# Sparse attention feeding an MLP mixer: the global part of PV on 64 by 64 quarters, PV tiles in pairs, leftovers and first transposes at other places of a period

## The chip, the cores and the metric

The kernel runs on one core of a Trainium2 chip. The metric is the device time of one execution in microseconds (us). The core has a matrix engine, TensorE (PE, with its weight loads shown apart as PEld), and three engines that work on tiles: VectorE (DVE), ScalarE (ACT) and GpSimd (POOL). SyncE (SP) issues most of the DMAs. PE's results land in PSUM, from where DVE and ACT take them to SBUF.

## What is computed

Eight batches of 576 tokens go through attention with eight heads of 64 numbers. A token sees the tokens within 32 places, eight global tokens see and are seen by all. The result, 576 by 512 per batch, goes through a token-mixing MLP and a channel-mixing MLP.

```python
scores = scale * np.matmul(q, k.transpose(0, 1, 3, 2))
mask = np.abs(pos[:, None] - pos[None, :]) <= window
mask = mask | is_global[:, None] | is_global[None, :]
scores = np.where(mask, scores, -1000000000.0)
attn = np.exp(scores - max); attn = attn / (sum + 1e-09)
x = np.matmul(attn, v)                       # heads side by side: 576 x 512
h = np.maximum(x.T @ w_tok1, 0.0) @ w_tok2   # tokens mixed: 576 -> 256 -> 576
u = x + h.T
out = u + np.maximum(u @ w_ch1, 0.0) @ w_ch2 # channels mixed: 512 -> 1536 -> 512
```

## The kernel before

**Tiles.** The 576 tokens of a batch are five token tiles, four of 128 and one of 64. Scores are kept with keys on partitions and queries in columns, in strips of 64 keys that cover a band, so that the exponentials (`e_all`) are the stationary operand of the product with V. Heads are handled in four pairs p. A batch's attention has these steps, with their lines:

- `cast_qk` (ACT, L386 and L383) makes 16-bit copies of q and k. `T(b, p)` (PE, L400) transposes a pair's q and k into one PSUM tile `pT`, and DVE copies it out as `qT` (L406) and `kT` (L412). `TR(b)` (PE, L427) does the same for the leftovers, the last 64 tokens of all heads, in PSUM tile `pr`, copied out at L438. `globals_` (L392) puts the global queries beside `qT`.
- `S_` (PE, L458) makes the scores of a pair in two PSUM tiles, ACT takes the exponential (L470), `SM` (DVE, L476 and L481) applies the masks.
- `GK` and `LX` make `lf`: 128 rows, 16 per head, against all tokens, the part of the attention that goes through global tokens. `OG` (L539, L544) makes its other operand `rf`: the same 128 rows by 8 heads x 66 columns. `rf` is zero outside a head's own 16 rows, so rows 0 to 63 hold heads 0 to 3 and rows 64 to 127 heads 4 to 7.
- `PV(b, tau)` forms token tile tau of the attention: for each half of the heads (`hf`), a global product `lf` by `rf` (L656, 264 columns), then the local products `e_all` by V (L665, 66 columns for each of four heads), all for two strips of 64 queries (`tiles`), one in each half of PE's columns. The fifth tile has one strip only. 66 columns are 64 of V, one of ones whose sum is the denominator, and one of padding. DVE takes the reciprocal (L678) and divides (L679) into `x`.

The mixer's steps are `M1` (L692, five parts `ch` over the token tiles, then ACT makes `a`), `M2` (L716, three parts; DVE adds x and writes `u`, L721, or `ul`, L724), `M3` (a DMA transpose of `u` on SP, L733), then the dense products `M4` (L754, `b1p`, ACT makes `b`, L757) with `M4l` (L767) for the fifth tiles of two batches together, and `M5` (L780, `op`; DVE adds, L784, SP stores).

**PSUM.** Three pools: `pss` has two slots of two banks, `psv` one slot of two banks, `psm` two slots of one bank. A tile waits for a slot's earlier user to be read. Scores, `a1p` of M1, `hp` of M2 and most transposes come from `pss`; GK, OG and even PV tiles from `psv`; M4 and M5 from `psm`.

**Order.** The order of work on each engine is the order in which the program calls these functions; nothing reorders it. The program runs in periods b = 0 to 7. Period b works off the dense products M4 and M5 of batch b, and beside them, in two halves, the attention end of batch n = b+1 (PV, M1, M2, M3) and the attention beginning of batch m = b+2 (casts, TR, T, S_, SM, GK, OG). `first_half` and `second_half` write the order of periods 2 to 6 by hand: a list in which each `D` stands for the next dense unit (one M4, four matmuls of 512 columns) and the rest are the steps named above. In `first_half`, `c(k)` are two casts, `pv(tau)` is PV(n, tau), `tt(p)` is T(m, p) with its copies. Periods 0 and 1 have their own lists (`period_0`, `sparse2`); in period 0 the PV tiles of batch 1 already stand in pairs. Period 6 has no batch m, period 7 is dense work alone.

Of the kernel before, what the change touches and what calls it, by code (L numbers as in the profile page):

```python
# [9 lines left out]
F16 = mybir.dt.float16  # L10
# [5 lines left out]
P = 128  # L16
# [5 lines left out]
HQ = 64  # L22
ES = QS * NT - HQ
VW = 66
# [20 lines left out]
def kernel(  # L45
# [13 lines left out]
    B, H, S, D = q.shape  # L59
# [4 lines left out]
    NP = H // 2  # L64
# [14 lines left out]
    def pss(shape, dtype=F32, name="s"):  # L79
        return psS.tile(shape, dtype, tag="s", name=name)  # L80
# [252 lines left out]
    def gather_t(t):  # L333
        pg = (psm if t == 0 else psv)([P, 2, P], F16, name=f"pg_{t}")
        for ti in range(2):
            if t > 0:
                nc.vector.tensor_copy(out=g16[ti][t], in_=g32[ti][t])
            nc.tensor.transpose(out=pg[:, ti, :], in_=g16[ti][t], identity=ident)
        st[0]["gt", t] = pg
        if t > 0:  # L340
            GTE(t)
            GKE(t)
# [45 lines left out]
    def casts(b):  # L388
        return [lambda ti=ti, p=p: cast_qk(b, ti, p, nc.scalar.copy) for p in (None, 0, 1, 2, 3) for ti in range(2)]
# [4 lines left out]
        )  # L394

    def T(b, p):
        pT = (psm if b in (0, 2) else pss)([P, 2, 512], F16, name=f"pT_{b}_{p}")
        for ti, n in enumerate((qn, kn)):
            for i in range(4):
                nc.tensor.transpose(  # L400
                    out=pT[:, ti, P * i : P * i + P], in_=n[b % 2][:, i, 2 * p : 2 * p + 2, :], identity=ident
                )
        st[b]["pT", p] = pT
# [15 lines left out]
        TEk(b, p)  # L419

    def TR(b):
        pr = (psm if b in (0, 2) else pss)([P, 2, 4, NP * 16], name=f"pr_{b}")
        sel = ident.rearrange("p (n r x) -> p r n x", n=NP, r=2)
        for ti, n in enumerate((qr, kr)):
            for i in range(4):
                for par in range(2):
                    nc.tensor.matmul(  # L427
                        pr[64 * par : 64 * par + 64, ti, i, :], lhsT=n[b % 2][:, i, :], rhs=sel[:, par], start=True, stop=True
                    )
        st[b]["pr"] = pr  # L430
        if b > 0:
            TRE(b)

    def TRE(b, tis=(0, 1), eng=nc.vector.tensor_copy):
        for ti in tis:
            v_ = st[b]["pr"][:, ti].rearrange("p i (n x) -> p n x i", n=NP)
            dst = qTs[b % 2][:, :, NT - 1, NG : NG + LAST] if ti == 0 else kTs[b % 2][:, :, WIN + 512 : WIN + S]
            eng(out=dst.rearrange("p n (x i) -> p n x i", i=4), in_=v_)  # L438
# [208 lines left out]
    def PV(b, tau):  # L647
        s = st[b]

        sh = 64 if tau == NT - 1 and b % 2 == 1 else 0  # L650
        tiles = ((2 * tau, 0), (2 * tau + 1, 64)) if tau < NT - 1 else ((2 * tau, sh),)
        ps = (pss if b != 2 and tau % 2 else psv)([P, 2, 512], name=f"pv_{b}_{tau}")

        def glob(hf):
            for t, r0 in tiles:
                nc.tensor.matmul(  # L656
                    ps[r0 : r0 + 64, hf, 0 : NP * VW], lhsT=s["lf"][:, HQ * t : HQ * t + HQ],
                    rhs=s["rf"][:, 2 * hf : 2 * hf + 2], start=True, stop=False,
                )

        def local(hf, hh):
            h = NP * hf + hh
            for t, r0 in tiles:
                lo = QS * tau + (NG + HQ if t % 2 else NG)
                nc.tensor.matmul(  # L665
                    ps[r0 : r0 + 64, hf, VW * hh : VW * hh + VW], lhsT=e_all[:, h, lo : lo + HQ],
                    rhs=(vod if t % 2 else vsh)[b % 2][:, tau, h, :],
                    start=False, stop=hh == NP - 1,
                )

        for hf in range(2):
            glob(hf)
            for hh in range(NP):
                local(hf, hh)
        r = slice(0, P) if tau < NT - 1 else slice(sh, sh + 64)
        pq = ps[:, :, 0 : NP * VW].rearrange("p f (h x) -> p f h x", h=NP)
        rr = tiny.tile([P, 2, NP], F32, tag="rr", name=f"rr_{b}_{tau}")
        nc.vector.reciprocal(out=rr[r], in_=pq[r, :, :, D])  # L678
        nc.vector.tensor_tensor(  # L679
            out=x16s[b % 2][r, tau, :].rearrange("p (f h x) -> p f h x", f=2, h=NP), in0=pq[r, :, :, 0:D],  # L680
            in1=rr[r].unsqueeze(3).to_broadcast([P if tau < NT - 1 else 64, 2, NP, D]), op=ALU.mult,
        )

    def M1(b, ch):
        s = st[b]
        if ch == 0:
            ps = pss([P, 2, 512], name=f"a1p_{b}")
            s["a1p"], s["a1pp"] = [ps[:, 0], ps[:, 1]], ps
        ps = s["a1p"]
        for tt in range(2):  # L690
            w = w1[:, ch, P * tt : P * tt + P] if ch < NT - 1 else w1l[:, b % 2, P * tt : P * tt + P]
            nc.tensor.matmul(ps[tt], lhsT=w, rhs=x16s[b % 2][:, ch, :], start=(ch == 0), stop=(ch == NT - 1))  # L692
        if ch < NT - 1:
            return
        a1 = mb.tile([P, 2, DM], F16, tag="a1", bufs=1, name=f"a1_{b}")
        if b == 1:
            nc.scalar.activation(out=a1[:, 0], in_=s["a1pp"][:, 0], func=AF.Relu)
            nc.vector.tensor_scalar(out=a1[:, 1], in0=s["a1pp"][:, 1], scalar1=0.0, scalar2=None, op0=ALU.max)
        else:
            nc.scalar.activation(out=a1, in_=s["a1pp"], func=AF.Relu)  # L700
        s["a1"] = a1
        s["u16"] = mb.tile([P, 4, DM], F16, tag="u16", name=f"u16_{b}")
        if b % 2 == 0:
            s["ul"] = mb.tile([P, DM], F16, tag="ul", name=f"ul_{b}")
        else:
            s["ul"] = st[b - 1]["ul"]

    def M2(b, part):
        s = st[b]
        x16 = x16s[b % 2]  # L710
        taus = ((0, 1), (2, 3), (4,))[part]
        ps = pss([P, 2, 512], name=f"hp_{b}_{part}")
        sh = 64 if (part == 2 and b % 2) else 0
        for i, tau in enumerate(taus):
            for ch in range(2):
                nc.tensor.matmul(  # L716
                    ps[:, i, :], lhsT=w2[:, ch, P * tau - sh : P * tau - sh + P], rhs=s["a1"][:, ch, :],
                    start=(ch == 0), stop=(ch == 1),
                )
        if part < 2:  # L720
            nc.vector.tensor_add(out=s["u16"][:, 2 * part : 2 * part + 2], in0=x16[:, 2 * part : 2 * part + 2], in1=ps)  # L721
        else:
            r = slice(sh, sh + 64)
            nc.vector.tensor_add(out=s["ul"][r], in0=x16[r, NT - 1], in1=ps[r, 0])  # L724

    def M3(b, part):
        s = st[b]
        if part == 0:
            s["uT"] = mb.tile([P, 4, 512], F16, tag="uT", name=f"uT_{b}")
        if part < 2:  # L730
            for i in range(2):
                tau = 2 * part + i
                nc.sync.dma_start_transpose(out=s["uT"][:, :, P * tau : P * tau + P], in_=s["u16"][:, tau, :])  # L733
        else:
            s["uTl"] = mb.tile([P, 4, P], F16, tag="uTl", name=f"uTl_{b}")
            nc.sync.dma_start_transpose(out=s["uTl"], in_=s["ul"])
# [54 lines left out]
    def t(b, p):  # L791
        T(b, p)
        TE(b, p)
# [58 lines left out]
    def first_half(b):  # L852
        n, m = b + 1, b + 2
        D = None
        cs = casts(m) if m < B else []

        def c(k):
            return cs[2 * k : 2 * k + 2]

        def tt(p):  # L860
            return [lambda: t(m, p)] if m < B else []

        def pv(tau):
            return lambda: PV(n, tau)

        if n == B:
            return []
        u = [D, D, pv(0), D, pv(1), *c(0), D, pv(2), *c(1), D, pv(3), lambda: [M1(n, ch) for ch in range(3)], *c(2), D]
        if b == 2:
            u += [lambda: gather_t(1)]  # L870
        u += [pv(4), *([lambda: TR(m)] if m < B else []), *tt(0), *c(3), D, lambda: M1(n, 3), D, lambda: M1(n, 4), *c(4)]
        if m < B:
            u += [lambda: load_v16(m), lambda: globals_(m)]
        if m + 1 < B:
            u += [lambda: (load_rest(m + 1), load_qk(m + 1, slice(0, H)))]
        u += [*tt(1), D, D, lambda: (M2(n, 0), M3(n, 0)), D, lambda: (M2(n, 1), M3(n, 1)), *tt(2), D]
        u += [lambda: (M2(n, 2), M3(n, 2) if n % 2 else None), D]
        return u

# [25 lines left out]
    masks_b()  # L905
    masks_c()
    T(0, 0)
    TEq(0, 0, A)
    cast_qk(0, 1, None, A)
# [166 lines left out]
```

## Time and profile before

| | us |
|---|---|
| median of 14 runs | 347.77 |
| lowest and highest of them | 345.51, 349.94 |
| the profiled execution's own time | 346.72 |
| its span, first to last instruction | 344.8 |
| PE busy | 314.2 |
| DVE busy | 191.9 |
| ACT busy | 156.0 |
| POOL busy | 64.7 |

The span's rows are in us from its start. A timeline row has the start, the length, the engine, the line, the operation, what it writes and reads, for PE the rows and columns of the array that the weights take (128\*64: 128 rows by 64 columns) and the moving operand's shape, then how many instructions the row merges, and in brackets how long the engine stood idle before it and what ended that. The end of a matmul is modelled, about 0.17 us after its last column has gone in, so following matmuls overlap in the rows, and the step from start to start says what PE's queue costs. The granted clock of TensorE was 0.988 of full speed over the span.

### The profile page before, as it was taken

Reading aid. Unit: us, or ns where it says so; the run is one execution under the profiler, and the core shown is the slowest. Engines: PE = TensorE matmul, PEld = TensorE weight load, DVE = VectorE, ACT = ScalarE, POOL = GpSimd, SP = SyncE. Lnnn points to the kernel's source line nnn. Section 1 sums busy time; section 2 is a strip of 40 time slices with the busy share of each in tenths; the row PEclk is TensorE's granted clock in tenths of the full one; section 3 lists DMA queues with packets and bytes.
Section 4 is the critical chain, followed back from the end, with each engine's and each line's share of the span. In section 5 each row is a group of like instructions: output and inputs, shape, how many; then the busy total and the mean of one; then the engine's idle time right before and its main releaser. Section 6 shows DMA issues by size and latency. Waiting matters only on the chain.

```text
span 344.8 us, 8245 instructions
## 1 busy us (share of the span) xinstructions
PE 314.2 (91%) x3505; PEld 172.6 (50%) x3505; DVE 191.9 (56%) x410; ACT 156.0 (45%) x281; POOL 64.7 (19%) x99
## 2 busy tenths in 40 slices
PE   4789997997899889799989999899989999999994
PEld 4557653545455535444445545444446545444641
DVE  7486448759744775466756384557756374231021
ACT  3460586514765156454455435554456433413600
POOL 5696588500030003100120003100000000000000
PEclk9997999999999999999999999999999999999999
DMA  7999999964795916779395816796102212042013
GB/s 209 201 129 211 281 183 246 211 69 70 253 89 130 250 63 72 59 243 141 74 89 181 155 64 96 66 253 136 58 0 22 73 67 59 2 108 90 2 61 91
DMA packets 78198, 41.85 MB, mean 121 GB/s; under 512 B 54482, under 2 KB 72274, under 8 KB 78162
## 3 DMA queue, kind: packets, MB, share of 16 engines
q1 hardware_dynamic: 39552, 28.45, 31.9%
q0 software_dynamic: 38608, 12.88, 31.0%
q8 instruction: 27, 0.44, 0.6%
q14 instruction: 9, 0.07, 0.1%
q10 hardware_dynamic: 2, 0.00, 0.0%
HBM read 36.11 MB, written 9.44 MB: 132 GB/s over the span
## 4 chain that ended last, share of the span: by engine, by line
PE 74%; DVE 16%; issue 5%; ACT 2%; POOL 1%; DVEq 0%; ACTq 0%
PE b1p L754 23%; PE op L780 22%; PE a1p L692 5%; PE hp L716 4%; PE pv L656 4%; PE b1lp L767 3%; PE pT L400 3%; PE s L458 3%; PE pv L665 3%; DVE vod L374 2%; DVE vod L373 1%; DVE osb L784 1%; DVE kT L412 1%; DVE e_all L481 1%; DVE x L679 1%
## 5 line engine op out<-in xcount | busy, mean ns | idle before, releaser
L757 ACT ACTIVATE b<-b1p 128x512 f16<-128x512 f32 x96 | 57.0, 598 | 87.9 <-PE b1p L754 87.8
L754 PE MATMUL b1p<-uT,wc 128*128 128x512 f16 x384 | 94.7, 380 | 0.8 <-ACT b L757 0.6
L780 PE MATMUL op<-wc,b 128*128 128x512 f16 x384 | 90.0, 380 | 0.0
L470 ACT ACTIVATE e_all<-s 128x544 f16<-128x544 f32 (+1 forms) x64 | 40.9, 686 | 39.8 <-issue 27.2
L361 POOL DMA_DIRECT2D vsh<-in_v_dram x35 | 30.0, 859 | 141.6 <-DVE rr L678 119.6
L780 PEld LDWEIGHTS <-b 128*128 128x128 f16 x384 | 35.0, 98 | 38.9
L754 PEld LDWEIGHTS <-wc 128*128 128x128 f16 x384 | 34.6, 98 | 37.9 <-issue 2.2
L784 DVE TENSOR_TENSOR osb<-u,op 128x512 f32<-128x512 f16 x32 | 21.9, 685 | 55.9 <-PE op L780 53.9
L406 DVE COPY qT<-pT 128x512 f16<-128x512 f16 x30 | 20.6, 686 | 13.5 <-PE pT L400 13.5
L721 DVE TENSOR_TENSOR u<-x,hp 128x1024 f16<-128x1024 f16 x14 | 17.0, 1221 | 17.5 <-PE hp L716 17.5
L678 DVE RECIPROCAL rr<-pv 128x8 f32<-128x8 f32 (+1 forms) x35 | 7.2, 207 | 33.6 <-PE pv L665 33.6
L481 DVE TENSOR_TENSOR e_all<-e_all,bandm 128x616 f16<-128x616 f16 x56 | 24.3, 476 | 1.0
L679 DVE TENSOR_TENSOR x<-pv,rr 128x512 f16<-128x512 f32 (+1 forms) x35 | 24.2, 691 | 1.2
L458 PE MATMUL s<-qT,kT 64*64 64x136 f16 (+2 forms) x704 | 17.7, 217 | 5.1 <-ACT e_all L470 1.6
L412 DVE COPY kT<-pT 128x512 f16<-128x512 f16 x30 | 20.4, 681 | 1.4 <-PE pT L400 0.9
L458 PEld LDWEIGHTS <-kT 64*64 64x64 f16 x704 | 11.4, 107 | 17.1 <-issue 12.2
L656 PE MATMUL pv<-rf,lf 128*64 128x264 f16 x126 | 18.9, 287 | 0.9 <-DVE kgz L355 0.7
L716 PE MATMUL hp<-a,w 128*128 128x512 f16 x72 | 18.9, 379 | 0.0
L400 PE MATMUL pT<-ident,qn 128*128 128x128 f16 x128 | 12.7, 223 | 6.5 <-DVE kT L438 6.3
L665 PE MATMUL pv<-vsh,e_all 128*64 128x66 f16 x280 | 18.5, 194 | 0.0
L665 PEld LDWEIGHTS <-e_all 128*64 128x64 f16 x504 | 18.4, 111 | 0.0
L386 ACT CAST qn<-lq 128x512 f16<-128x512 f32 x27 | 16.5, 613 | 3.2 <-DMA lq<-in_q_dram 3.2
(175 smaller groups left out, 363.9 us busy)
## 6 DMA issues: line engine op xcount, KB each, us to landing
out_dram<-osb SPq DMA_DIRECT2D x32, 256.0 KB
lq<-in_q_dram SPq DMA_DIRECT2D x5, 1024.0 KB
lk<-in_k_dram SPq DMA_DIRECT2D x5, 1024.0 KB
wc<-in_moe_w_ch_dram POOLq DMA_DIRECT2D x6, 512.0 KB, 13.8
vsh<-in_v_dram POOLq DMA_DIRECT2D x21, 128.0 KB, 4.9
lq<-in_q_dram POOLq DMA_DIRECT2D x2, 1024.0 KB, 10.6
lk<-in_k_dram POOLq DMA_DIRECT2D x2, 1024.0 KB, 11.8
vsh<-in_v_dram POOLq DMA_DIRECT2D x14, 96.0 KB, 3.5
```

Source lines behind the costliest of these rows:

```text
L361: nc.gpsimd.dma_start(out=vsh[b % 2][r0:r1, c, :, 0:D], in_=v[b, :, j0 : j0 + (r1 - r0), :].rearrange("h p d -> p h d"),)
L458: nc.tensor.matmul(ps[o, par, i0 - a : i1 - a], lhsT=kT[r, HQ * j : HQ * j + HQ], rhs=qf[r, i0:i1], start=b > 0, stop=b > 0 or j in js[-2:],)
L470: nc.scalar.activation(out=e2[:, :, a:z], in_=ps[:, :, 0 : z - a], func=AF.Exp, scale=scale)
L481: nc.vector.tensor_mul(out=e2[:, par], in0=e2[:, par], in1=bm)
L656: nc.tensor.matmul(ps[r0 : r0 + 64, hf, 0 : NP * VW], lhsT=s["lf"][:, HQ * t : HQ * t + HQ], rhs=s["rf"][:, 2 * hf : 2 * hf + 2], start=Tr ...
L665: nc.tensor.matmul(ps[r0 : r0 + 64, hf, VW * hh : VW * hh + VW], lhsT=e_all[:, h, lo : lo + HQ], rhs=(vod if t % 2 else vsh)[b % 2][:, tau ...
L679: nc.vector.tensor_tensor(out=x16s[b % 2][r, tau, :].rearrange("p (f h x) -> p f h x", f=2, h=NP), in0=pq[r, :, :, 0:D], in1=rr[r].unsquee ...
L716: nc.tensor.matmul(ps[:, i, :], lhsT=w2[:, ch, P * tau - sh : P * tau - sh + P], rhs=s["a1"][:, ch, :], start=(ch == 0), stop=(ch == 1),)
L754: nc.tensor.matmul(ps, lhsT=wc1[:, cc, P * j : P * j + P], rhs=s["uT"][:, cc, :], start=(cc == 0), stop=(cc == 3))
L757: nc.scalar.activation(out=s["b1"][:, j, :], in_=ps, func=AF.Relu)
L780: nc.tensor.matmul(ps, lhsT=w, rhs=wc2[:, j, :], start=(j == 0), stop=(j == NJ - 1))
L784: nc.vector.tensor_add(out=osb, in0=s["u16"][:, tau], in1=ps)
```

## The change

Three things are edited.

- In `PV`, the global product of a half of the heads takes only the 64 rows in which `rf` is not zero for it, rows 64 hf to 64 hf + 63, so that with two strips of queries its four matmuls lie on the four 64 by 64 quarters of PE. All four are issued first, then the local products of both halves.
- In `first_half`, PV tiles 0 and 1, and 2 and 3, follow each other without a dense unit between them. `TR(m)` and `tt(0)` to `tt(2)` stand later and apart from each other.
- From batch 3 on, `TR` and the transposes of pairs 1 and 3 take their PSUM from `psv` instead of `pss`.

```diff
     def T(b, p):
-        pT = (psm if b in (0, 2) else pss)([P, 2, 512], F16, name=f"pT_{b}_{p}")
+        pT = (psm if b in (0, 2) else psv if b > 2 and p % 2 else pss)([P, 2, 512], F16, name=f"pT_{b}_{p}")
...
     def TR(b):
-        pr = (psm if b in (0, 2) else pss)([P, 2, 4, NP * 16], name=f"pr_{b}")
+        pr = (psm if b in (0, 2) else psv if b > 2 else pss)([P, 2, 4, NP * 16], name=f"pr_{b}")
...
         def glob(hf):
+            g = slice(HQ * hf, HQ * hf + HQ)
             for t, r0 in tiles:
                 nc.tensor.matmul(
-                    ps[r0 : r0 + 64, hf, 0 : NP * VW], lhsT=s["lf"][:, HQ * t : HQ * t + HQ],
-                    rhs=s["rf"][:, 2 * hf : 2 * hf + 2], start=True, stop=False,
+                    ps[r0 : r0 + 64, hf, 0 : NP * VW], lhsT=s["lf"][g, HQ * t : HQ * t + HQ],
+                    rhs=s["rf"][g, 2 * hf : 2 * hf + 2], start=True, stop=False,
                 )
...
+        glob(0)
+        glob(1)
         for hf in range(2):
-            glob(hf)
             for hh in range(NP):
                 local(hf, hh)
...
-        u = [D, D, pv(0), D, pv(1), *c(0), D, pv(2), *c(1), D, pv(3), lambda: [M1(n, ch) for ch in range(3)], *c(2), D]
+        u = [D, D, pv(0), pv(1), *c(0), D, *c(1), D, pv(2), pv(3), *c(2), D, lambda: [M1(n, ch) for ch in range(3)], D]
         if b == 2:
             u += [lambda: gather_t(1)]
-        u += [pv(4), *([lambda: TR(m)] if m < B else []), *tt(0), *c(3), D, lambda: M1(n, 3), D, lambda: M1(n, 4), *c(4)]
+        u += [pv(4), *c(3), D, lambda: M1(n, 3), D, *([lambda: TR(m)] if m < B else []), lambda: M1(n, 4), *c(4)]
...
-        u += [*tt(1), D, D, lambda: (M2(n, 0), M3(n, 0)), D, lambda: (M2(n, 1), M3(n, 1)), *tt(2), D]
+        u += [D, *tt(0), D, lambda: (M2(n, 0), M3(n, 0)), D, *tt(1), lambda: (M2(n, 1), M3(n, 1)), D, *tt(2)]
         u += [lambda: (M2(n, 2), M3(n, 2) if n % 2 else None), D]
```

The order on the engines, in period b=3 (batch n=4, batch m=5). First PE from the first PV tile on, before; the last number of a name is a running number, `b1p` is a dense unit.

```order
L656 MATMUL pv_0_2867<-rf_2852,lf_2780 64x264
...
L665 MATMUL pv_0_2867<-vsh_91,e_all 64x66
...
L754 MATMUL b1p_2_2891<-uT_2581,wc_195 128x512
...
L656 MATMUL pv_1_2897<-rf_2852,lf_2780 64x264
...
L754 MATMUL b1p_3_2923<-uT_2581,wc_195 128x512
...
L656 MATMUL pv_2_2929<-rf_2852,lf_2780 64x264
```

The same place of PE in the change:

```order
L657 MATMUL pv_0_2867<-rf_2852,lf_2780 64x264
...
L666 MATMUL pv_0_2867<-vsh_91,e_all 64x66
...
L657 MATMUL pv_1_2891<-rf_2852,lf_2780 64x264
...
L756 MATMUL b1p_2_2917<-uT_2570,wc_195 128x512
...
L756 MATMUL b1p_3_2925<-uT_2570,wc_195 128x512
...
L657 MATMUL pv_2_2931<-rf_2852,lf_2780 64x264
```

PV tile 1 has moved up against tile 0, and the two dense units that stood behind one tile each now follow both. Next PE around the leftovers (`pr`) and the first transposes (`pT_0`), before:

```order
L656 MATMUL pv_4_3000<-rf_2852,lf_2780 64x264
...
L427 MATMUL pr_3014<-ident,qr_88 64x64
...
L400 MATMUL pT_0_3033<-ident,qn_84 128x128
...
L754 MATMUL b1p_6_3046<-uT_2581,wc_195 128x512
...
L692 MATMUL a1p_2985<-x_0_216,w_192 128x512
...
L754 MATMUL b1p_7_3054<-uT_2581,wc_195 128x512
...
L692 MATMUL a1p_2985<-x_0_216,w1l 128x512
```

The same place of PE in the change:

```order
L657 MATMUL pv_4_3000<-rf_2852,lf_2780 64x264
...
L756 MATMUL b1p_6_3016<-uT_2570,wc_195 128x512
...
L694 MATMUL a1p_2987<-x_0_216,w_192 128x512
...
L756 MATMUL b1p_7_3024<-uT_2570,wc_195 128x512
...
L427 MATMUL pr_3030<-ident,qr_88 64x64
...
L694 MATMUL a1p_2987<-x_0_216,w1l 128x512
...
L756 MATMUL b1p_8_3067<-uT_2570,wc_195 128x512
...
L400 MATMUL pT_0_3073<-ident,qn_84 128x128
```

Two dense units and part 3 of M1 now stand between PV tile 4 and the leftovers, part 4 of M1 and one more dense unit between the leftovers and the first transposes. Last DVE from the end of PV tile 4 to the end of M2, before:

```order
L679 TENSOR_TENSOR x_0_216<-pv_4_3000,rr_4_3011 64x512
L438 CAST qT_139<-pr_3014 128x4x64
L438 CAST kT_141<-pr_3014 128x4x64
L406 COPY qT_139<-pT_0_3033 128x4x128
L412 COPY kT_141<-pT_0_3033 128x512
L392 COPY qT_139<-gT 128x20x8
L406 COPY qT_139<-pT_1_3078 128x4x128
L412 COPY kT_141<-pT_1_3078 128x512
L721 TENSOR_TENSOR u_4_3064<-x_0_216,hp_0_3101 128x1024
L721 TENSOR_TENSOR u_4_3064<-x_0_216,hp_1_3116 128x1024
L406 COPY qT_139<-pT_2_3124 128x4x128
```

The same place of DVE in the change:

```order
L681 TENSOR_TENSOR x_0_216<-pv_4_3000,rr_4_3011 64x512
L438 CAST qT_139<-pr_3030 128x4x64
L438 CAST kT_141<-pr_3030 128x4x64
L392 COPY qT_139<-gT 128x20x8
L406 COPY qT_139<-pT_0_3073 128x4x128
L412 COPY kT_141<-pT_0_3073 128x512
L723 TENSOR_TENSOR u_4_3053<-x_0_216,hp_0_3090 128x1024
L406 COPY qT_139<-pT_1_3105 128x4x128
L412 COPY kT_141<-pT_1_3105 128x512
L723 TENSOR_TENSOR u_4_3053<-x_0_216,hp_1_3116 128x1024
L406 COPY qT_139<-pT_2_3130 128x4x128
```

On DVE the first addition `u` now comes ahead of the copies of `pT_1`, and those stand between the two additions. On POOL and SP no row changes its place. On ACT some of the dense units' activations (L757) and the casts change places with each other.

## The prediction

> **What bounds the kernel now.** I read the page's head and its chain first, then the waits of PE, then the timeline of one period, engine by engine. The page says that PE is nearly always busy and that the chain which ends last runs through PE for three quarters of its length, mostly through the two dense products (L754, L780).
>
> ```profile
> span 344.8 us, 8245 instructions
> PE 314.2 (91%) x3505; PEld 172.6 (50%) x3505; DVE 191.9 (56%) x410; ACT 156.0 (45%) x281; POOL 64.7 (19%) x99
> ...
> PE 74%; DVE 16%; issue 5%; ACT 2%; POOL 1%; DVEq 0%; ACTq 0%
> ```
>
> So what shortens PE's own queue shortens the end, and what PE waits for is the first thing to look at. The waits of PE (line, awaited engine and line: total, times, longest) have one at the top, on exactly the lines that the change moves.
>
> ```profile
> PE pT L400 <- DVE kT L438: 6.3, 4, 1.7
> ...
> PE s L458 <- DVE kT L412: 1.4, 4, 0.4
> ...
> PE b1p L754 <- ACT b L757: 0.6, 2, 0.4
> ```
>
> Its four times are the four periods b=2 to 5, in which leftovers and transposes of another batch are placed. One of them, b=3, on PE (start, length, line, what):
>
> ```profile
> 170.18 0.30 PE L656 MATMUL pv<-rf,lf 128*64 128x264 f16 x2
> ...
> 170.78 1.04 PE L754 MATMUL b1p<-uT,wc 128*128 128x512 f16 x4
> 171.75 0.30 PE L656 MATMUL pv<-rf,lf 128*64 128x264 f16 x2
> ...
> 176.19 0.30 PE L656 MATMUL pv<-rf,lf 128*64 128x264 f16 x1
> ...
> 178.62 0.38 PE L400 MATMUL pT<-ident,qn 128*128 128x128 f16 x4 [1.51 <-DVE kT L438]
> ...
> 179.06 1.03 PE L754 MATMUL b1p<-uT,wc 128*128 128x512 f16 x4
> 179.92 0.60 PE L692 MATMUL a1p<-x,w 128*128 128x512 f16 x2
> ```
>
> Here a dense unit D (four 512-column matmuls) takes 179.92 - 179.06 = 0.86 us, so 0.42 ns a column, and T(m,0), eight transposes, 179.06 - 178.62 = 0.44. One PV tile with its D takes 171.75 - 170.18 = 1.57, so 0.71 of it is PV and the changes of array shape around it. The transposes at 178.62 stood 1.51 us idle behind PV tile 4 and the leftovers, which have nothing dense between them.
>
> **The wait that goes: -6.3 us.** In the change two D and part of M1 stand between PV tile 4 and the leftovers, the leftovers use the other PSUM pool, and M1's end and a D stand between them and T(m,0). T(m,0) starts at least M1(4) 0.43 + D 0.86 = 1.3 after the leftovers. Its buffer is then tile 3's, emptied long before. The whole 6.3 us go. The leftovers now wait for tile 4's division instead, some 1.2 us after its last matmul, but D, M1(3), D = 2.15 us lie between: covered by 0.9.
>
> **What is late next: +1.4 us.** The copies do not vanish, they move down the DVE queue to between the additions u (L721). The last token part, M2(2), needs the buffer of the second u. On DVE and PE in the same period:
>
> ```profile
> 178.07 0.40 DVE L438 CAST kT<-pr 128x256 f16<-128x256 f32 x1
> 179.26 0.69 DVE L406 COPY qT<-pT 128x512 f16<-128x512 f16 x1 [0.79 <-PE pT L400]
> 179.87 0.68 DVE L412 COPY kT<-pT 128x512 f16<-128x512 f16 x1
> ...
> 184.89 1.22 DVE L721 TENSOR_TENSOR u<-x,hp 128x1024 f16<-128x1024 f16 x1 [1.30 <-PE hp L716]
> 186.62 1.22 DVE L721 TENSOR_TENSOR u<-x,hp 128x1024 f16<-128x1024 f16 x1 [0.51 <-PE hp L716]
> ```
>
> ```profile
> 183.82 1.03 PE L716 MATMUL hp<-a,w 128*128 128x512 f16 x4
> ...
> 186.86 1.03 PE L754 MATMUL b1p<-uT,wc 128*128 128x512 f16 x4
> 187.89 0.59 PE L716 MATMUL hp<-a,w 128*128 128x512 f16 x2
> ```
>
> Now M2(2) starts at 187.89, 0.17 after its D is done (186.86 + 0.86), on the second u, which ends at 187.84. For the change I count from the end of M1(4). PE runs D to 0.86, T(m,0) to 1.30, D to 2.16, M2(0) to 3.02, D to 3.88, T(m,1) to 4.32, M2(1) to 5.18, D to 6.04, T(m,2) to 6.48, and M2(2) is next. DVE starts copies 0.64 after a T starts (178.62 to 179.26), 0.61 apart, and u 1.07 after its M2 starts (183.82 to 184.89). So u(0) runs from 3.23 to 4.45, the copies of T(m,1) from 4.52 to about 5.8, u(1) from 5.75 to 6.97. M2(2) starts at 7.02 and waits 0.54, against 0.17 now: +0.35 or so a period, four times, 1.4. The other end of this is zero, if u(1) passes in time, and about +1.2 a period if one more pair of copies comes ahead of it.
>
> **A PSUM slot that comes free: -0.8 and -1.05 us.** T(m,3) moves to the other pool, so the scores after it no longer wait for its copies. Two strips of scores without and with that wait:
>
> ```profile
> 153.74 0.46 PE L458 MATMUL s<-qT,kT 64*64 64x72 f16 x22
> 154.13 1.47 PE L780 MATMUL op<-wc,b 128*128 128x512 f16 x6
> ...
> 157.27 0.65 PE L458 MATMUL s<-qT,kT 64*64 64x72 f16 x22
> 157.86 0.39 PE L780 MATMUL op<-wc,b 128*128 128x512 f16 x1
> ```
>
> 0.59 against 0.39 us: 0.2 in each of four periods. Batch 3's transposes, at the end of period b=1, profit more:
>
> ```profile
> 116.72 0.39 PE L400 MATMUL pT<-ident,kn 128*128 128x128 f16 x4
> 116.81 0.68 DVE L412 COPY kT<-pT 128x512 f16<-128x512 f16 x1
> ...
> 117.55 0.31 PE L458 MATMUL s<-qT,kT 64*64 64x72 f16 x10 [0.44 <-DVE kT L412]
> ...
> 118.64 0.35 PE L458 MATMUL s<-qT,kT 64*64 64x72 f16 x12 [0.78 <-ACT e_all L470]
> ```
>
> Now the first part waits for the copy of T(3,2) (116.81 + 0.68 = 117.49), the second for the exp of the first, since T(3,3) holds the other slot. In the change the first part starts when T(3,3) is through, near 117.04. The second then takes over the wait for that same copy and starts at about 117.6 instead of 118.64: -1.05. What follows there is led by these scores, on DVE and ACT as well.
>
> **PV itself: -1.5 us for the pairs, +0.8 for leftovers set apart.** The inside of a PV tile:
>
> ```profile
> 62.36 0.30 PE L656 MATMUL pv<-rf,lf 128*64 128x264 f16 x2
> ...
> 62.49 0.19 PE L665 MATMUL pv<-vsh,e_all 128*64 128x66 f16 x1
> ...
> 62.62 0.28 PE L656 MATMUL pv<-rf,lf 128*64 128x264 f16 x2
> ...
> 63.31 0.20 PE L665 MATMUL pv<-vod,e_all 128*64 128x66 f16 x1
> 63.44 1.47 PE L780 MATMUL op<-wc,b 128*128 128x512 f16 x6
> ```
>
> The global block holds PE 0.13 us (62.36 to 62.49; 264 columns alone are 0.11), four pairs of local matmuls another 0.13. From the last local matmul to the dense one pass 0.13 where pairs follow at 0.03: a change of array shape costs 0.10. The dense matmuls of the D above show the same price on the way in: 171.75 - 170.78 = 0.97 for 0.86 of work. Does it also fall due where only the rows change, 64 to 128, as it now must inside every PV tile? And do four 64 by 64 quarters run at once? The nearest rows:
>
> ```profile
> 26.24 0.25 PE L587 MATMUL pv<-rf,lf 32*64 32x66 f16 x4
> 26.42 0.22 PE L579 MATMUL pv<-vsh,e_all 128*64 128x66 f16 x1
> ...
> 120.32 0.31 PE L458 MATMUL s<-qT,kT 64*64 64x72 f16 x10
> 120.56 0.39 PE L780 MATMUL op<-wc,b 128*128 128x512 f16 x1
> ```
>
> Four 66-column matmuls of 32 rows need 0.06 in two pairs, 0.12 in a row, yet the first of 128 rows comes 0.18 after: a price between 0.06 and 0.12, so I take 0.10. In the scores ten matmuls of 72, 136, 136, 136 and 64 columns for two heads, 1088 columns or 0.46 us in a row, take 0.24 - 0.10 = 0.14: four at a time. So the quarters' block takes 0.13 instead of two of 0.12 each, but pays 0.10 for the change to the local matmuls: a tile takes 0.13 + 0.10 + 0.26 + 0.10 = 0.59, against 0.61 now. **The quarters alone are worth almost nothing.** The pairs gain: two tiles with their way in cost 2 x 0.71 = 1.42 now and 0.10 + 2 x 0.59 = 1.28 then, about 0.15 for each of ten pairs (b=2 to 6). Tile 4 and the leftovers, now both of 64 columns and next to each other, are set apart by dense work: two more changes of shape, 0.2 in four periods. Batches 1 and 2 keep their order: 0.
>
> The ends for the block never shown: 0.11 (its columns alone) and 0.44 (four in a row). I take 0.13, near the scores' row. For the inner change: 0 and 0.12.
>
> One rule of the Trainium skill speaks against the block: TensorE: Matmul & The Clock Gate, Part 3, says that a weight load overlaps running matmuls only where the row group differs, and here the two blocks of one row group follow each other. The row at 62.36 disagrees: two matmuls of one row group, 528 columns, let the next start after 0.13 and not 0.22 us. By the rule the sum would be the first rival's.
>
> **Sum.** -6.3 + 1.4 - 0.8 - 1.05 - 1.5 + 0.8 = -7.45 us. The profiled execution took 346.72 us with its span of 344.8; that gives 339.3. The median of the runs shown is 347.77, 1.05 above this execution, so I put the forecast at **340.3 us**. Three things I cost at nothing. ACT's casts and activations: PE waits for b only 0.6 us in the whole run (third row of the waits), and in the walk above every dense unit's buffer is free 0.1 us or more ahead; without that cover each late activation costs its own delay. The copy of the global queries (L392, 0.2 us) moves ahead of T(m,0)'s copies on DVE, which has time there. And the DMA transposes on SP:
>
> ```profile
> 186.14 5.84 SPq L733 DMA_TRANSPOSE uT<-u x4
> ```
>
> They follow u and land some 0.8 us later against M1(4) than now, but their reader is the next period, behind four token tiles of M5 (48 matmuls of 512 columns, 10 us). SP's and POOL's own order does not change.
>
> **Rivals.**
> 1. The quarters run only two at a time. Each of 35 PV tiles (7 batches, 5 tiles) then pays 0.11 more: +3.9, 344.2. Against it the scores' row; for it, that no row shows this order of quarters. 0.09.
> 2. The inner change of shape is free. 35 inside tiles and 12 between tiles of a pair, 0.10 each: -4.7, 335.6. Against it the row at 26.42. 0.07.
> 3. DVE becomes the bound behind M2: the copies come in front of both u, or the scores wait for T(m,2)'s. +0.6 in four periods: 342.7. For it, that DVE is left without a gap from T(m,1) on; against it, that it was idle 1.30 and 0.51 before the two u. 0.15.
> 4. The wait only changes its place: the leftovers stand still for tile 4's division as T(m,0) did for them. Nothing of 6.3 is won: 346.6. Against it the cover of 0.9. 0.04.
> 5. Slower: the quarters run one after the other, 0.44 instead of 0.13 in each of 35 tiles: +10.9, 351.2. It decides once the block takes more than 0.13 + 9.2/35 = 0.39 us. Against it stand the ten score matmuls in 0.14. 0.03.
>
> My forecast has 0.62. The range reaches to the first and third rival and half way to the second: 336.0 to 344.3. About 0.5% (1.7 us) is what a measurement of this kernel can tell from no change. Faster by more than that: forecast and rivals 1 to 3, less a remainder for what nobody listed, 0.92; same 0.05; slower 0.03.
>
> **What would show it.** Right: no wait of L400 for L438 in periods b=2 to 5; one PV pair with its way in at 1.28; M2(2) with a wait of about 0.5 for u; score strips of 0.39 everywhere in the second halves; 118.64's counterpart a microsecond nearer to the transposes. Wrong: a gap in front of the leftovers (rival 4); first local matmul of a tile more than 0.3 after the first quarter (rivals 1, 5) or less than 0.15 (rival 2); M2(2) waiting over 1 us (rival 3). The forecast falls if anything else takes PE's place in the chain within the shortened periods, above all DVE.

## The result and the profile after

The changed kernel took 340.0 us (median of 10 runs, 338.47 to 344.15), the kernel before 347.25 (47 runs). The ratio of the runs is 0.978, with a 95% interval from 0.975 to 0.982; it leaves out runs more than 1.5% above the fastest of their kernel, such as the one of 344.15. The forecast was 340.3.

The head and the chain of the changed kernel's page. All lines of the kernel after `glob` stand one or two numbers higher now: L656 is L657, L665 L666, L679 L681, L716 L718, L721 L723, L754 L756, L780 L782.

```profile
span 339.8 us, 8241 instructions
PE 317.4 (93%) x3505; PEld 172.6 (51%) x3505; DVE 193.2 (57%) x410; ACT 155.8 (46%) x281; POOL 63.8 (19%) x99
...
PE 77%; DVE 14%; ACT 3%; issue 2%; DMA 2%; DVEq 0%; ACTq 0%
```

PE still carries the chain, with a larger share of a shorter span. The waits of PE in the changed kernel (line, awaited engine and line: total, times, longest):

```profile
PE hp L718 <- DVE u L723: 1.3, 4, 0.3
...
PE s L458 <- DVE kT L412: 1.2, 4, 0.4
PE s L458 <- ACT e_all L470: 0.8, 1, 0.8
```

The row of 6.3 us, L400 for L438, is gone. A new row of four waits has come, M2's last part for the second u. The waits of L458 lie before period 2 in both kernels. The same period as in the prediction, b=3, on PE:

```profile
168.06 0.31 PE L657 MATMUL pv<-rf,lf 64*64 64x264 f16 x4
168.29 0.22 PE L666 MATMUL pv<-vsh,e_all 128*64 128x66 f16 x1
168.30 0.22 PE L666 MATMUL pv<-vod,e_all 128*64 128x66 f16 x1
168.35 0.20 PE L666 MATMUL pv<-vsh,e_all 128*64 128x66 f16 x1
...
168.67 0.31 PE L657 MATMUL pv<-rf,lf 64*64 64x264 f16 x4
...
169.28 1.90 PE L756 MATMUL b1p<-uT,wc 128*128 128x512 f16 x8
...
178.34 0.32 PE L427 MATMUL pr<-ident,qr 128*64 128x64 f16 x8
...
180.02 0.39 PE L400 MATMUL pT<-ident,qn 128*128 128x128 f16 x4
...
185.45 0.39 PE L400 MATMUL pT<-ident,kn 128*128 128x128 f16 x4
186.17 0.59 PE L718 MATMUL hp<-a,w 128*128 128x512 f16 x2 [0.33 <-DVE u L723]
```

Leftovers (178.34) and first transposes (180.02) start without a wait. M2's last part starts at 186.17, where the transposes before it were through at 185.45 + 0.22 = 185.67: it stands 0.50 us (the 0.33 in the row is counted from the modelled end of the transposes, which is 0.17 later). The reason on DVE, in the same kernel:

```profile
183.70 0.69 DVE L406 COPY qT<-pT 128x512 f16<-128x512 f16 x1
184.31 0.68 DVE L412 COPY kT<-pT 128x512 f16<-128x512 f16 x1
184.91 1.21 DVE L723 TENSOR_TENSOR u<-x,hp 128x1024 f16<-128x1024 f16 x1
```

No idle time stands before the second u, which ends at 186.12: the two copies of T(m,1) came first.

To see what each period gained I take the start of a batch's first dense matmul to that of the next batch's. For b=3 these are the rows at 166.55 and 207.81 before, 166.00 and 205.89 in the changed kernel, first the kernel before, then the changed one:

```profile
166.55 2.13 PE L754 MATMUL b1p<-uT,wc 128*128 128x512 f16 x8
...
207.81 1.53 PE L754 MATMUL b1p<-uT,wc 128*128 128x512 f16 x6
```

```profile
166.00 2.13 PE L756 MATMUL b1p<-uT,wc 128*128 128x512 f16 x8
...
205.89 0.81 PE L756 MATMUL b1p<-uT,wc 128*128 128x512 f16 x3
```

41.26 us have become 39.89. The same for every period and for the experiments below, as the difference to the kernel before, in us:

| kernel | b=1 | b=2 | b=3 | b=4 | b=5 | b=6 | time, ratio to before (95%) |
|---|---|---|---|---|---|---|---|
| changed | -1.04 | -1.51 | -1.36 | -1.52 | -1.35 | -0.17 | 0.978 (0.975 to 0.982) |
| e1_quarters | +0.05 | +0.05 | +0.04 | +0.04 | +0.05 | +0.04 | 1.004 (1.000 to 1.008) |
| e2_no_quarters | -1.09 | -1.81 | -1.66 | -1.80 | -1.65 | -0.46 | 0.976 (0.971 to 0.982) |
| e3_pools | -1.09 | +0.93 | -0.56 | -0.68 | -0.56 | 0.00 | 0.990 (0.986 to 0.993) |
| e4_order | 0.00 | -1.62 | -1.47 | -1.61 | -1.46 | -0.46 | 0.982 (0.976 to 0.988) |
| e5_strip_order | -1.04 | -1.50 | -1.36 | -1.51 | -1.35 | -0.17 | one run, 337.82 us beside 346.88 |
| e6_pair_blocks | -1.09 | -1.99 | -1.85 | -2.00 | -1.84 | -0.66 | 0.973 (0.967 to 0.979) |
| e7_tr_t2 | -1.09 | -2.51 | -2.37 | -2.52 | -2.37 | -0.45 | 0.969 (0.964 to 0.974) |
| e8_all | -1.09 | -2.71 | -2.56 | -2.72 | -2.56 | -0.66 | 0.964 (0.959 to 0.970) |

The first dense matmul and period b=0 are left out of the table: together they differ by -1.9 to +2.0 us between these executions, for a reason told at the end. Period 7 differs nowhere by more than 0.02. Each entry comes from one execution of its kernel. So the periods tell the effects apart to some hundredths of a microsecond where the times can't to better than one.

### The profile page after: what moved, and what is told of

Read it like the earlier page. It is cut to its first block, busy times and chain, and to the rows that moved or that the text cites. A ratio compares the mean times of both kernels' runs of the same rounds, so it can differ in the third digit from the quotient of the medians.

```text
span 339.8 us, 8241 instructions
## 1 busy us (share of the span) xinstructions
PE 317.4 (93%) x3505; PEld 172.6 (51%) x3505; DVE 193.2 (57%) x410; ACT 155.8 (46%) x281; POOL 63.8 (19%) x99
## 4 chain that ended last, share of the span: by engine, by line
PE 77%; DVE 14%; ACT 3%; issue 2%; DMA 2%; DVEq 0%; ACTq 0%
PE op L782 23%; PE b1p L756 21%; PE a1p L694 5%; PE pv L666 4%; PE hp L718 4%; PE b1lp L769 3%; PE s L458 3%; PE pv L657 2%; PE pT L400 2%; PE warm L208 2%; DVE kT L412 2%; DMA lq<-in_q_dram 2%; DVE osb L786 2%; DVE qT L406 2%; DVE vod L373 1%
## 5 line engine op out<-in xcount | busy, mean ns | idle before, releaser
L756 PE MATMUL b1p<-uT,wc 128*128 128x512 f16 x384 | 94.5, 380 | 0.8 <-ACT b L759 0.6
L782 PE MATMUL op<-wc,b 128*128 128x512 f16 x384 | 90.0, 380 | 0.0
L756 PEld LDWEIGHTS <-wc 128*128 128x128 f16 x384 | 35.0, 98 | 40.0 <-issue 2.2
L782 PEld LDWEIGHTS <-b 128*128 128x128 f16 x384 | 35.1, 98 | 38.8
L681 DVE TENSOR_TENSOR x<-pv,rr 128x512 f16<-128x512 f32 (+1 forms) x35 | 24.2, 691 | 1.2
L723 DVE TENSOR_TENSOR u<-x,hp 128x1024 f16<-128x1024 f16 x14 | 17.0, 1218 | 12.1 <-PE hp L718 12.1
L718 PE MATMUL hp<-a,w 128*128 128x512 f16 x72 | 18.9, 379 | 1.3 <-DVE u L723 1.3
L458 PE MATMUL s<-qT,kT 64*64 64x136 f16 (+2 forms) x704 | 17.1, 217 | 2.8 <-DVE kT L412 1.2
L458 PEld LDWEIGHTS <-kT 64*64 64x64 f16 x704 | 11.1, 107 | 14.4 <-issue 11.5
L386 ACT CAST kn<-lk 128x512 f16<-128x512 f32 x27 | 16.8, 622 | 0.9 <-DMA lk<-in_k_dram 0.9
L666 PE MATMUL pv<-vsh,e_all 128*64 128x66 f16 x280 | 15.5, 197 | 0.0
L694 PE MATMUL a1p<-x,w 128*128 128x512 f16 x56 | 14.2, 379 | 0.0
L666 PEld LDWEIGHTS <-e_all 128*64 128x64 f16 x504 | 11.7, 110 | 4.3
```

Of the source, the lines that this page charges most:

```text
L386: eng(out=(qn, kn)[ti][b % 2][:, :, hs].rearrange("p i h d -> p h i d"), in_=(lq, lk)[ti][:, hs])
L458: nc.tensor.matmul(ps[o, par, i0 - a : i1 - a], lhsT=kT[r, HQ * j : HQ * j + HQ], rhs=qf[r, i0:i1], start=b > 0, stop=b > 0 or j in js[-2:],)
L666: nc.tensor.matmul(ps[r0 : r0 + 64, hf, VW * hh : VW * hh + VW], lhsT=e_all[:, h, lo : lo + HQ], rhs=(vod if t % 2 else vsh)[b % 2][:, tau ...
L718: nc.tensor.matmul(ps[:, i, :], lhsT=w2[:, ch, P * tau - sh : P * tau - sh + P], rhs=s["a1"][:, ch, :], start=(ch == 0), stop=(ch == 1),)
L756: nc.tensor.matmul(ps, lhsT=wc1[:, cc, P * j : P * j + P], rhs=s["uT"][:, cc, :], start=(cc == 0), stop=(cc == 3))
L782: nc.tensor.matmul(ps, lhsT=w, rhs=wc2[:, j, :], start=(j == 0), stop=(j == NJ - 1))
```

## The experiments

**Each edit alone, and the change without the quarters.** The change has three edits, quarters, order and pools. Four kernels take them apart. First the quarters alone, on the kernel before:

```diff
+            g = slice(HQ * hf, HQ * hf + HQ)
...
-                    ... lhsT=s["lf"][:, HQ * t : HQ * t + HQ], rhs=s["rf"][:, 2 * hf : 2 * hf + 2], ...
+                    ... lhsT=s["lf"][g, HQ * t : HQ * t + HQ], rhs=s["rf"][g, 2 * hf : 2 * hf + 2], ...
...
+        glob(0)
+        glob(1)
         for hf in range(2):
-            glob(hf)
```

> The kernel before with the first edit alone: PV's global part on four quarters, all four first. Theory (the quarters pay a change of array shape inside every tile and win nothing): a single tile 0.61 us against 0.60 before, the pair of tiles that batch 1 already has 1.23 against 1.09, period b=0 longer by 0.3 to 0.4, all others within 0.1; time 0 to +0.7 us. Rival (the quarters are a good part of the gain, one block of 0.11 us saved in each of 35 tiles): -3.5 us or so, ratio 0.990.

Ratio 1.004, every period of the table a little longer. One PV tile of this kernel on PE, single:

```profile
169.49 0.31 PE L657 MATMUL pv<-rf,lf 64*64 64x264 f16 x4
...
170.11 1.04 PE L756 MATMUL b1p<-uT,wc 128*128 128x512 f16 x4
```

0.62 us from the first quarter to the dense matmul behind, against 0.60 to 0.61 before. Period b=0 grew by 0.48, where 0.3 to 0.4 was expected, but the period itself can't show it: in kernels whose b=0 is that of the kernel before it differs by 0.02 (e8_all) to 3.82 us (e2_no_quarters). Its PV tiles can. Batch 1's already stood in pairs, 63.44 - 62.36 = 1.08 us before; with quarters, here in the changed kernel, the first pair takes 65.29 - 64.06 = 1.23:

```profile
64.06 0.31 PE L657 MATMUL pv<-rf,lf 64*64 64x264 f16 x4
...
65.29 1.04 PE L782 MATMUL op<-wc,b 128*128 128x512 f16 x4
```

That is 0.15 more for each of two pairs. The quarters bring nothing; the rival's -3.5 us are out.

Next the changed kernel without the quarters, that is the same diff the other way round.

> The changed kernel without the first edit: order and PSUM pools as changed, PV's global part as before. Theory: a pair of tiles takes 1.09 us plus 0.09 on the way in, against 1.23 plus 0.09 in the changed kernel, so 0.14 less for each of 12 pairs; sum over the periods -8.3 us against before, where the changed kernel has -6.6; ratio 0.976 or lower. Rival (the quarters help): slower than the changed kernel by 2 us or more, ratio 0.985.

The time, 0.976, can't be told from the changed kernel's 0.978, but each of the periods b=2 to 6 is 0.28 to 0.30 us shorter than in the changed kernel. The pair of tiles:

```profile
166.72 0.30 PE L656 MATMUL pv<-rf,lf 128*64 128x264 f16 x2
...
167.81 1.90 PE L754 MATMUL b1p<-uT,wc 128*128 128x512 f16 x8
```

1.09 us where the changed kernel has 169.28 - 168.06 = 1.22. The sum expected, -8.3, is -8.47 over periods 1 to 6. Period 6, in which only the pairs differ from before, says what the pairs alone are worth: 0.46 without quarters, 0.17 with them.

Then the PSUM pools alone, on the kernel before.

```diff
-        pT = (psm if b in (0, 2) else pss)([P, 2, 512], F16, name=f"pT_{b}_{p}")
+        pT = (psm if b in (0, 2) else psv if b > 2 and p % 2 else pss)([P, 2, 512], F16, name=f"pT_{b}_{p}")
...
-        pr = (psm if b in (0, 2) else pss)([P, 2, 4, NP * 16], name=f"pr_{b}")
+        pr = (psm if b in (0, 2) else psv if b > 2 else pss)([P, 2, 4, NP * 16], name=f"pr_{b}")
```

> The kernel before with the third edit alone: leftovers and odd transposes of batches 3 to 7 in the other PSUM pool, order as before. Theory: the leftovers, right behind PV tile 4, now wait for its division (some 1.2 us), the first transposes follow at once; 0.3 us gained there in each of periods b=2 to 5, 0.2 more at the score strips, and 1.05 in period b=1: -3 us, ratio 0.991. Rival (a missing PSUM slot is the whole cause of the wait, the place in the order does not matter): -1.6 and -0.2 in each of four periods and -1.05, together -8 us.

Period 1 gains its microsecond from this edit alone. In periods 3 to 5 the gain is 0.6 to 0.7, not the 1.8 of the rival: most of the wait only changed its place. The waits of PE in this kernel:

```profile
PE pr L427 <- DVE x L679: 4.1, 4, 1.0
```

The leftovers stand four times behind PV tile 4 for its division. This is what the prediction's fourth rival describes. Period 2 is even longer than before, by 0.93. There two waits of PE, 0.68 and 1.03 us, lie within 2.4 us, and behind them the granted clock fell:

```profile
137.10 0.30 PE L656 MATMUL pv<-rf,lf 128*64 128x264 f16 x1 [0.68 <-DVE kgz L355]
...
138.80 0.36 PE L427 MATMUL pr<-ident,qr 128*64 128x64 f16 x8 [1.03 <-DVE x L679]
...
140.13 1.91 PE L754 MATMUL b1p<-uT,wc 128*128 128x512 f16 x4
```

```profile
136.00:138.70 2.70, 1.09 (x14) 0.68 (x12) 1.43 (x5) 1.62 (x3) 0.63 (x1) 1.00 1.11 68
138.70:142.20 3.50, 3.40 (x29) 2.02 (x30) 2.29 (x6) 0.12 (x1) 0.15 (x1) 0.53 0.44 28
142.20:146.00 3.80, 3.80 (x25) 1.96 (x24) 1.29 (x2) 2.89 (x5) 0.00 (x0) 0.98 0.00 0
```

The second fence is the same kernel by stretches; the last three numbers of a row are the granted clock (1.00, 0.53, 0.98), the DMA share and GB/s. A dense unit whose row says 1.03 elsewhere says 1.91 there. This is one execution. The kernel before has even longer waits at the same place, 0.68 and 1.66 us, with the clock at 1.00; so that the two waits lowered it is not shown.

Last the order alone, on the kernel before: the new lists of `first_half`, as in the change's diff.

> The kernel before with the second edit alone: the new order of first_half, pools and PV as before. Theory: the first transposes no longer wait (-1.58 a period in b=2 to 5), pairs -0.45, leftovers apart +0.19, the last part of M2 waits 0.5 for u (+0.35) and the second part a little for the first u (+0.2), score strips as before: -1.3 in each of four periods, -0.45 in b=6, nothing in b=0 and 1; -5.6 us, ratio 0.984. Rival (without the other pool the copies hold the PSUM slots and the wait only moves): less than 0.5 a period, ratio above 0.993.

-1.46 to -1.62 a period, -0.46 in b=6, nothing in b=1, ratio 0.982. The wait of L400 is gone without the other pool, so the place in the order was its cause. The row of waits on u is smaller here than with the pools:

```profile
PE hp L716 <- DVE u L721: 0.7, 4, 0.2
```

M2 stands as long as with the pools all the same, but in two places, since its second part waits too:

```profile
180.66 0.39 PE L400 MATMUL pT<-ident,kn 128*128 128x128 f16 x4
181.04 1.02 PE L716 MATMUL hp<-a,w 128*128 128x512 f16 x4
...
182.99 0.39 PE L400 MATMUL pT<-ident,kn 128*128 128x128 f16 x4
183.55 0.59 PE L716 MATMUL hp<-a,w 128*128 128x512 f16 x2 [0.17 <-DVE u L721]
```

The second part starts 181.04 - (180.66 + 0.22) = 0.16 late, the last 183.55 - (182.99 + 0.22) = 0.34: together 0.50, as in the changed kernel. I had put the 0.2 of the second part on top of a full 0.5 for the last. That is the 0.2 by which the gain came out larger than the 1.3 expected.

**Why the quarters win nothing.** Two causes could be separated: the change of array shape inside the tile, or quarters that hinder each other. The first kernel visits the changed kernel's quarters in another order.

```diff
-        def glob(hf):
-            g = slice(HQ * hf, HQ * hf + HQ)
-            for t, r0 in tiles:
+        for t, r0 in tiles:
+            for hf in range(2):
+                g = slice(HQ * hf, HQ * hf + HQ)
                 nc.tensor.matmul(
```

> The changed kernel with the four quarters of a tile in the other order: both head halves of one strip of queries, then of the next, so that neighbours differ in rows of the array and not in columns. Theory (all four run at once in either order, the 0.24 us from the first quarter to the first local matmul are 0.11 of columns and a change of shape): block and tile as in the changed kernel, 0.24 and 0.61 us, periods b=2 to 6 within 0.1 of it. Rival (quarters of one row group hinder each other's weight loads): the block shorter by 0.02 to 0.11, up to 0.5 us a period.

Periods and pairs are those of the changed kernel (the pair 165.49 - 164.26 = 1.23), and so is the step from the first quarter to the first local matmul (164.50 - 164.26 = 0.24, in the changed kernel 168.29 - 168.06 = 0.23):

```profile
164.26 0.31 PE L657 MATMUL pv<-rf,lf 64*64 64x264 f16 x4
164.50 0.22 PE L666 MATMUL pv<-vsh,e_all 128*64 128x66 f16 x1
...
165.49 1.90 PE L754 MATMUL b1p<-uT,wc 128*128 128x512 f16 x8
```

The order of the quarters does not matter. The rule on row groups that the prediction named beside its first rival (the Trainium skill, TensorE: Matmul & The Clock Gate, Part 3) shows no effect here. The order alone does not tell four quarters at once with a change of shape, 0.13 + 0.10, from quarters two at a time with a free change, 0.22 by their columns. The second kernel does. It lets one change of shape serve two tiles; single tiles have whole columns again.

```diff
+    def PVg(b, tau):          # allocates a tile's PSUM and issues its four quarters
...
-        u = [D, D, pv(0), pv(1), *c(0), D, *c(1), D, pv(2), pv(3), *c(2), D, ...
+        def pair(tau):
+            return lambda: (PVg(n, tau), PVg(n, tau + 1), PV(n, tau), PV(n, tau + 1))
+
+        u = [D, D, pair(0), *c(0), D, *c(1), D, pair(2), *c(2), D, ...
```

> Order and pools as changed; in the pairs of periods b=2 to 6 the eight quarters of both tiles come first, then all local matmuls, so that one change of shape inside serves two tiles; single tiles as before the change. Theory (what spoils the quarters is one change of shape a tile): a pair takes 1.0 us, against 1.09 with whole columns and 1.23 in the changed kernel; b=2 to 6 each 0.15 shorter than in e2_no_quarters. Rival (the quarters themselves run slower than their columns say): a pair no shorter than 1.09.

A pair takes 0.98 us, and periods 2 to 6 are 0.18 to 0.20 shorter than in e2_no_quarters:

```profile
164.97 0.42 PE L654 MATMUL pv<-rf,lf 64*64 64x264 f16 x8
...
165.95 1.90 PE L770 MATMUL b1p<-uT,wc 128*128 128x512 f16 x8
```

In the first row eight quarters are merged. The second four by themselves, and the first local matmul:

```profile
165.10 0.28 PE L654 MATMUL pv<-rf,lf 64*64 64x264 f16 x4
165.32 0.22 PE L680 MATMUL pv<-vsh,e_all 128*64 128x66 f16 x1
```

The first four hold PE for 165.10 - 164.97 = 0.13 us, the same as the prediction's block, so four do run at once. From the second four to the local matmuls pass 0.22: 0.09 more, the change of shape. Two at a time with a free change is out. Used in this way the quarters do pay. The change of shape was their price.

**A version without the costs that are left.** Two costs of the change were left: the two shape changes around the leftovers and the wait on u. The next kernel is e2_no_quarters with the leftovers back behind PV tile 4, in `pss`, and T(m,2) behind M2's last part, in `psv`.

```diff
-        u += [pv(4), *c(3), D, lambda: M1(n, 3), D, *([lambda: TR(m)] if m < B else []), lambda: M1(n, 4), *c(4)]
+        u += [pv(4), *([lambda: TR(m)] if m < B else []), *c(3), D, lambda: M1(n, 3), D, lambda: M1(n, 4), *c(4)]
...
-        u += [D, *tt(0), ..., D, *tt(1), lambda: (M2(n, 1), M3(n, 1)), D, *tt(2)]
-        u += [lambda: (M2(n, 2), M3(n, 2) if n % 2 else None), D]
+        u += [D, *tt(0), ..., D, *tt(1), lambda: (M2(n, 1), M3(n, 1)), D]
+        u += [lambda: (M2(n, 2), M3(n, 2) if n % 2 else None), *tt(2), D]
```

> e2_no_quarters with two more moves in periods b=2 to 5: leftovers again right behind PV tile 4, in the first PSUM pool, but the first transposes still two dense units later; and T(m,2) behind M2's last part, in the second pool. Theory: the wait that went hung on the first transposes' place alone; leftovers save two changes of shape (0.19 a period), and M2's last part no longer waits for the second u (0.5): 0.7 less than e2_no_quarters in each of four periods, 2.8 in all, ratio near 0.968. Rival (the copies delay something else as much): no shorter than e2_no_quarters.

0.70 to 0.72 less in each of four periods. The leftovers stand where they stood before the change, in the same pool too, and no wait of L400 or L427 comes back: the wait that went hung on the place of the first transposes alone. M2's last part follows its dense unit at once, and the transposes follow it:

```profile
179.87 1.03 PE L754 MATMUL b1p<-uT,wc 128*128 128x512 f16 x4
180.74 0.59 PE L716 MATMUL hp<-a,w 128*128 128x512 f16 x2
181.17 0.39 PE L400 MATMUL pT<-ident,qn 128*128 128x128 f16 x4
```

With the pair blocks added:

> e7_tr_t2 with the pair blocks of e6_pair_blocks. Theory: both add up, 0.7 + 0.15 less than e2_no_quarters in each of b=2 to 5 and 0.15 in b=6; ratio near 0.966.

Ratio 0.964 (0.959 to 0.970), below the changed kernel's interval; the steps add up to within 0.02 us in the periods.

## Why the prediction came out right, step by step

- **The wait that goes, -6.3 us.** Right, in mechanism and size. e4_order shows that the place in the order does it, e3_pools that the other pool alone turns it into a wait for the division, as the fourth rival had it. In the changed kernel that wait is covered.
- **What is late next, +1.4.** Right: M2's last part waits 0.50 us, where the walk gave 0.54. e7_tr_t2 takes this wait and the shape changes away and gains both.
- **The free PSUM slot, -0.8 and -1.05.** Right. e3_pools has -1.09 in b=1. In the changed kernel the second part of batch 3's first scores starts 119.61 - 118.78 = 0.83 us after the last transposes, where it was 118.64 - 116.72 = 1.92:

```profile
118.78 0.39 PE L400 MATMUL pT<-ident,kn 128*128 128x128 f16 x4
...
119.61 0.34 PE L458 MATMUL s<-qT,kT 64*64 64x72 f16 x12 [0.20 <-DVE kT L412]
```

  The score strips of the second halves, here in the changed kernel, have no wait:

```profile
156.91 0.46 PE L458 MATMUL s<-qT,kT 64*64 64x72 f16 x22
157.31 1.04 PE L782 MATMUL op<-wc,b 128*128 128x512 f16 x4
```

  0.40 from start to start, as expected. Against e4_order, e2_no_quarters has 0.19 less in each of four periods, with the same 0.50 at M2, which agrees with the 0.2.
- **PV, -1.5 for the pairs.** Mechanism right, size too large. A tile was put at 0.59 and has 0.61: the first local matmul starts 0.23 after the first quarter (168.29 - 168.06), as foreseen from block and shape change, but the second pair of local matmuls follows the first after 0.06 and not 0.03. The gain for a pair is then 1.42 - (0.10 + 1.22) = 0.10, not 0.15. Period 6, where only two pairs count, has -0.17 where -0.3 was worked out, so some 0.09 a pair and -0.9 for ten.
- **Batches 1 and 2 keep their order: 0.** This was the term overlooked. Batch 1's pairs, before 1.08 each without a change of shape inside, now pay for two: 1.23, +0.3 for both. The single tiles of batch 2 lose 0.01 each (e1_quarters has +0.05 in b=1).
- **Leftovers set apart, +0.8.** Not seen by itself. e7_tr_t2 takes it away together with the wait on u: 0.70 a period, of which the wait is 0.50 by the row at 186.17. 0.2 is left for it, as put.
- **Sum.** -7.45 was worked out. The periods 1 to 6 show -6.95, and batch 1's pairs add 0.3, so some -6.65. The term that was mis-sized is the pairs' -1.5, and batch 1's 0.3 was left out. The medians differ by 7.25; with an interval of 0.975 to 0.982, 6.3 to 8.7 us of 347.25, the time can't tell these sums apart. That the measured median came within 0.3 us of the forecast is luck. The lower end of the range does not fit its own words: half way from 340.3 to the second rival is 338.0, not 336.0; the 340.0 measured lies above both.
- **Rivals.** The first and the fifth (quarters two at a time or one after the other) are out by the 0.13 of the first four quarters in e6_pair_blocks, the second (no price inside) by the 0.09 there, the third by the single wait of 0.5. The fourth is real, but only where the pools change and the order does not.

## What to carry to other kernels

A narrower tile of the array that halves the columns streamed is not a gain if it puts one more change of array shape into each unit of work: here 0.11 us saved met about as much paid, and only where one change served two tiles was something left. When a wait between two engines is taken away by putting work between, follow the other engine's queue to the next place where its result is wanted, and count there before and after. And where a buffer pool and an order are changed together, try each alone: here the pool alone moved most of the wait, the order alone removed it.

## What the runs showed beside this

**The start sets the noise.** What came before period 1 differed by up to 3.5 us between executions of kernels that are the same there (e3_pools and e8_all). Part of it is the clock: in some executions PE ran at about half clock for some microseconds in the first 50, at changing times, in others not at all. By stretches (the third number from the end is the granted clock), first the kernel before, then the changed kernel, then e3_pools:

```profile
30.00:37.00 7.00, 7.00 (x99) 6.39 (x96) 3.36 (x7) 0.80 (x3) 4.16 (x8) 0.56 1.14 285
```

```profile
27.00:38.00 11.00, 10.51 (x148) 9.32 (x148) 5.47 (x10) 1.15 (x3) 4.69 (x8) 0.57 1.13 265
```

```profile
30.00:44.00 14.00, 12.99 (x160) 8.66 (x161) 6.26 (x13) 6.96 (x13) 8.74 (x15) 1.00 1.13 268
```

The changed kernel's profiled execution was one of those with the longest stretch at half clock, and its first dense matmul came 1.6 us later than in the kernel before (41.20 against 39.60). So its span fell by only 5.0 us where its periods gained 6.6 (the 6.95 less the 0.40 that its b=0 was longer). I had not expected that a kernel whose PE is busy 91% of the time takes so much of its scatter, 344.9 to 350.1 us, from there. In 22 executions of the kernel before, those beside e1_quarters, the mean granted clock, 0.977 to 1.000, and the time have a correlation of -0.83; where in those executions the clock was low, no trace shows.

**The clock can fall in the middle too.** In e3_pools two waits of together 1.7 us within 2.4 were followed by 3.5 us at 0.53 of full speed, and the period, with a gain of half a microsecond or more in its neighbours, had a loss of 0.9. I saw it in one execution of one kernel, and the kernel before kept its clock through longer waits, so the cause stays open.
